# First batch's q and k transposed by half rows, pair 0's masks moved behind its keys, token weights moved ahead of values 3, and mode changes counted when the order is planned

## The chip, the cores and the metric

The kernel runs on one core of a Trainium2 chip. The core has a matmul engine (PE, whose weight loads are listed apart as PEld), a vector engine (DVE), a scalar engine (ACT), a general engine (POOL, which here also issues most loads and makes their descriptors in software) and a queue engine (SP, which issues the first loads and all stores). The metric is the device time of one execution in microseconds (us), as the median of several.

## What is computed

Attention with a sliding window of 128 keys and four "sink" keys that everyone sees, for 4 batches, 8 heads, 768 positions and 64 columns a head; its output, heads side by side as 512 columns, goes into an MLP mixer. Cut to what matters:

```python
scores = (q @ k.T) / sqrt(D)
keep = (pos_k < n_sink) | ((pos_q - pos_k >= 0) & (pos_q - pos_k < window))
x = softmax(where(keep, scores, -1e9)) @ v            # heads become columns: x is 768 x 512
h = relu(x.T @ w_tok1) @ w_tok2                       # token mixing, 768 -> 256 -> 768
u = x + h.T
out = u + relu(u @ w_ch1) @ w_ch2                     # channel mixing, 512 -> 1536 -> 512
```

## The kernel before, in words

**Tiling.** Two heads make a pair; 4 batches of 4 pairs give pairs 0 to 15. For a pair, q and k (128 rows by 6 blocks by 2 heads by 64 columns) are cast to bfloat16, transposed by PE into PSUM, and evicted to qT and kT by ACT or DVE. The two heads lie on the two halves of the 128 rows, so a score matmul contracts 64 rows and the two heads' matmuls use different halves of the array. Scores are made transposed, in three groups g of two key tiles each, so that exp(scores) is at once the stationary operand pT of the values matmul. Here "64-row" or "half-row" work is a matmul or transpose that uses half of the array's rows, and "128-row" work one that uses all.

**Masks.** For batch 0, `masked` (line 469) first writes large negative numbers into the score bank by a 128-row matmul of `mask_add` with the identity, two matmuls a group, and the scores accumulate on top. For later batches DVE multiplies pT by a 0/1 mask after the exponential (line 510).

**Sinks.** `score_sinks` (line 527) scores the sink keys of two pairs at once; their exponentials are pT_sink. `pv` (line 548) makes the values of half a pair with its sums, and DVE divides (recip, line 567, and norm, line 571).

**PSUM.** Two double banks called "sc" hold scores; four banks called "mx" hold everything else: transposes, sink scores, values, token mixing and channel mixing.

**Token and channel mixing.** `mix_h` and `mix_u` (lines 668 and 696) do token mixing for column groups g = 0 (pairs 0 and 1 of a batch) and g = 1 (pairs 2 and 3); u comes either by a DVE add of x or, with `by_pe`, by one more matmul of x with the identity, after which ACT or DVE only copies. u is transposed (`transpose_u`, line 757), and `mix_channels` (line 849) multiplies by w_ch1 and w_ch2.

**Transposes.** For batch 0 and for pair 4, `transpose_whole` (line 430) turns q or k by six 128-row transposes into one "mx" bank. For pair 0 it also issues 3 (q) and 4 (k) matmuls of a tile of ones, whose result nobody reads (`keep_warm`, line 138); seven more such matmuls open the kernel. From pair 5 on, `transposed` (line 448) turns q and k by 12 half-row transposes each, in one "sc" bank, in the same burst as the pair's first scores.

**What sets the order.** The instructions' order on every engine is worked out while the kernel is built. `Plan` (line 236) holds when each engine is free by a table of costs; units of PE work have dependencies and PSUM banks (`unit`, line 352; `burst`, line 361, puts pieces together and adds 190 ns). `Plan.run` (line 306) takes, among the lists of batch 0 (scores, masks, transposes, values, token mixing of g = 1, of g = 0), the first that can start within 40 ns of the soonest; after that the channel units ("main") and the later batches' attention and token units ("side") alternate, so that the side keeps to `target` (line 1022), a share of its total size. Evictions and other work go to the engine that ends first, and `urgent` settles ties. POOL's queue of loads follows the order of the `queue` calls (lines 961 to 1000): values 1, 2, 3, then w_tok1, w_tok2, then pair 4, two pieces of w_ch1, pair 5, and so on; at most 8 loads are under way. The plan's landing time of a weight load counts 2000 ns for it in the queue (`load_weights`, line 953).

Of the kernel before, what the change touches and what calls it, by code (L numbers as in the profile page):

```python
# [16 lines left out]
def kernel(  # L17
# [13 lines left out]
    nc = tc.nc  # L31
# [14 lines left out]
    NQ = 6  # L46
    MASKED_BY_PE = 4

# [163 lines left out]
    SEM = 90.0  # L212
    PE_OUT = 190.0
    FIRST = 1800.0
    LANES = 8
# [5 lines left out]
    class Op:  # L221
        def __init__(self, cost, fn, deps=(), then=(), size=0.0, lag=None, loads=0):
            self.cost, self.fn, self.deps, self.then = cost, fn, list(deps), list(then)
            self.done = None
            self.lag = SEM if lag is None else lag
            self.size = size
            self.urgent = 0
            self.loads = loads
            self.need = {}

    def landed(at):
# [4 lines left out]
    class Plan:  # L236
        def __init__(self):
            self.free = {"PE": 0.0, "ACT": 0.0, "DVE": 0.0, "SP": 0.0, "POOL": 0.0}
            self.queue, self.landings = 0.0, []
            self.pending = []  # L240
            self.held = {t: [()] * n for t, n in TAGS.items()}
# [54 lines left out]
        def commit_pe(self, op, t):  # L296
            for tag, banks in op.need.items():
                given[tag] = [n for _, n in self.slots(tag)[:len(banks)]]
                for n, readers in zip(given[tag], banks):
                    self.held[tag][n] = readers  # L300
            op.fn()
            self.free["PE"] = t + op.cost["PE"]
            op.done = self.free["PE"] + PE_OUT + SEM
            self.pending.extend(op.then)

        def run(self, first, main, side, target):
# [3 lines left out]
            while any(first) or main or side or self.pending:  # L310
# [40 lines left out]

    def unit(ns, fn, deps=(), need=None, then=()):
# [5 lines left out]
        op.need = need or {}  # L358
        return op

    def burst(*pieces):
# [6 lines left out]
        def run():  # L368
# [19 lines left out]
    def prepare(p):  # L388

        kT, ks = kTb[p % NKB], kTs[p % NHP]  # L390
        parts = 2 if p < NHP else 1

        def evict(e, n, part):
            name = ("q", "k")[n]
            if n:
                t = kT
            elif ("qT", p) in tiles:
                t = tiles["qT", p]
            else:
                t = tiles["qT", p] = att_pool.tile([P, S], BF16, name="qT2")  # L400
            view, ps = tiles["ps_" + name, p]
            to = view(t)
            if parts == 2:
                ps, to = ps[:, ts(part, P // 2)], to[:, ts(part, P // 2)]
            copy(e, to, ps)

        def sink_columns(e):
            c = ODD * (p % 2)
            ps = tiles["ps_k", p][1]
            first = ps[:, 0, 0:n_sink] if len(ps.shape) == 3 else ps[:, 0, 0, 0:n_sink]  # L410
            for i in range(2):
# [7 lines left out]
        for n, name in enumerate(("qT", "kT")):  # L419
# [3 lines left out]
            for part, op in enumerate(done[name, p]):  # L423
                op.urgent = (3 - part if parts == 2 else 0)
        tiles["kT", p] = kT
# [3 lines left out]

    def transpose_whole(p, n):  # L430

        name = ("q", "k")[n]

        def run():
            ps = bank("mx", NT, P, dtype=BF16)
            tiles["ps_" + name, p] = (
                lambda t: t.rearrange("d (p j) -> d p j", j=NT), ps.rearrange("d j p -> d p j"),
            )
# [5 lines left out]
        then = done[name + "T", p] + ([done["kTs", p]] if n else [])  # L444
        done["t" + name, p] = unit(340, run, [done[name + "_bf", p]], {"mx": [then]}, then)
        return done["t" + name, p]

    def transposed(p):

        def run():  # L450
            ps = bank("sc", 2, 8 * P, dtype=BF16)[:, :, 0:2 * NT * D].rearrange("d x (n j p) -> d x n j p", n=2, j=NT)
            for n in range(2):
                for j in range(NT):
                    for x in range(2):
                        rows = ds(D * x, D)
                        in_order(nc.tensor.transpose(ps[:, x, n, j], bfs[p, n][rows, j], ident[rows, rows]))  # L456
                tiles["ps_" + "qk"[n], p] = (
                    lambda t: t.rearrange("d (x p j) -> d x p j", x=2, j=NT), ps[:, :, n].rearrange("d x j p -> d x p j"),
                )
# [9 lines left out]
    def masked(p, g):  # L469
# [78 lines left out]
    def pv(p, half):  # L548
# [230 lines left out]
    def first_attention():  # L779

        for p in range(NHP):
            prepare(p)
        turned = [transpose_whole(p, n) for p in range(NHP) for n in range(2)]
        masks, scored, out = [], [], []
        for p in range(NHP):
            for g in range(NT // 2):
                if p < MASKED_BY_PE:
                    masks.append(masked(p, g))
                if g == 0 or p < MASKED_BY_PE:
                    scored.append(burst(scores(p, g)))  # L790
                elif g == 1:
                    scored.append(burst(scores(p, 1), scores(p, 2)))
                if g == 0 and p == NHP - 1:
# [6 lines left out]
        for g in range(2):  # L800
            tokens.append([mix_h(0, g, t, 1) for t in range(NTOK)] if g else [mix_h(0, g, 0, NTOK)])
            tokens[g] += [mix_u(0, g, st, 2, st == 2) for st in range(0, NT, 2)]
            tokens[g] += [transpose_u(0, g, st, 2) for st in range(0, NT, 2)]
        return scored, masks, turned, out, *tokens[::-1]

    def attention_and_tokens():
# [3 lines left out]
        prepare(first)  # L810
        units += [transpose_whole(first, n) for n in range(2)]
        for p in range(first, last + 1):
# [140 lines left out]
    def load_weights(fn):  # L953
        return Op({"POOL": 760.0}, lambda e: fn(), lag=2000.0, loads=1)

# [114 lines left out]
```

## Time and profile before

| | us |
|---|---|
| median of 3 executions | 211.01 |
| lowest, highest | 210.95, 213.33 |
| profiled execution, device time | 211.41 |
| its span, first to last instruction | 209.6 |

How to read the lines below: a line of the timeline gives the start, the time until the end of the last instruction of the group, engine, source line, operation and "out<-in" by tile names, the shape and the count; in brackets stands how long the engine idled before it and what ended that. Since matmuls are pipelined, the time of one includes its way through the array; the spacing of starts is what one costs. A line of the stretches gives busy time and instruction count by engine. A line of the DMA view gives a load's size and the time from issue to landing. The chain is followed back from the last instruction, at each step to what released it.

### The profile page before, as it was taken

To read this page: it belongs to the slowest core of one execution; us is meant where nothing else is said; L and a number is where in the kernel's file an instruction comes from. 1 tells how busy PE (TensorE), PEld (TensorE's weight loads), DVE (VectorE), ACT (ScalarE), POOL (GpSimd) and SP (SyncE) were. 2 spreads that over 40 slices of the span, in tenths; PEclk is the share of its full clock that TensorE was granted. 3 is DMA by queue.
4 is the path that set the end of the run, shared out by engine and by line. 5 is a ranking of instruction groups with operands and counts; after the bars stand their busy time and mean duration, and the time that the engine had idled before them with its cause. 6 is when DMAs were issued, how large, how long until landed. Compare 5 with 4: busy or idle time off the path is not lost.

```text
span 209.6 us, 4916 instructions
## 1 busy us (share of the span) xinstructions
PE 200.8 (96%) x2071; PEld 122.2 (58%) x2090; DVE 114.7 (55%) x250; ACT 112.6 (54%) x200; POOL 67.4 (32%) x86
## 2 busy tenths in 40 slices
PE   7999999999999998999999999999999999999994
PEld 2555786565656565657656554666766545565443
DVE  4687554657677758876586452776663522000222
ACT  4697667958726435966684340968581102774000
POOL 6199849696599990630000000000000000000000
PEclk9999999999999999999999999999999999999999
DMA  6999999999999999793000212100001122000222
GB/s 193 281 250 177 170 177 189 150 146 195 165 172 194 184 185 199 52 83 27 0 3 2 103 50 100 53 0 5 0 3 50 50 103 100 0 0 3 100 100 100
DMA packets 73221, 21.55 MB, mean 103 GB/s; under 512 B 63216, under 2 KB 70256, under 8 KB 73200
## 3 DMA queue, kind: packets, MB, share of 16 engines
q0 software_dynamic: 67232, 11.80, 71.8%
q1 hardware_dynamic: 5968, 9.45, 12.7%
q8 instruction: 16, 0.26, 0.5%
q14 instruction: 5, 0.04, 0.1%
HBM read 26.75 MB, written 6.29 MB: 158 GB/s over the span
## 4 chain that ended last, share of the span: by engine, by line
PE 90%; ACT 5%; DVE 3%; issue 1%; ACTq 0%
PE ps_mx L109 77%; PE ps_sc L109 8%; PE ps_mx L112 2%; DVE kT L118 2%; PE ps_sc L456 2%; ACT qT L116 2%; ACT v1T L122 1%; ACT pT L506 1%; PE ps_mx L742 1%; ACT kTs L116 1%; DVE u_sb L713 0%; DVE ones L136 0%; PE ps_sc L742 0%; DVE o_sb L920 0%; ACTq L116 0%
## 5 line engine op out<-in xcount | busy, mean ns | idle before, releaser
L109 PE MATMUL ps_mx<-uT,w_ch 128*128 128x384 bf16 x384 | 67.4, 326 | 1.0 <-ACT v1T L122 0.9
L109 PE MATMUL ps_mx<-w_ch,v1T 128*128 128x512 bf16 (+2 forms) x298 | 64.4, 362 | 0.8 <-issue 0.2
L122 ACT ACTIVATE v1T<-ps_mx 128x384 bf16<-128x384 f32 x73 | 35.8, 492 | 30.4 <-PE ps_mx L109 20.1
L109 PEld LDWEIGHTS <-w_ch 128*128 128x128 bf16 x384 | 36.2, 98 | 24.8 <-issue 2.0
L109 PEld LDWEIGHTS <-v1T 128*128 128x128 bf16 x312 | 29.1, 98 | 29.5
L506 ACT ACTIVATE pT<-ps_sc 128x1024 bf16<-128x1024 f32 (+1 forms) x48 | 44.1, 951 | 2.9 <-PE ps_sc L109 2.6
L884 DVE TENSOR_TENSOR o_sb<-ps_mx,u_sb 128x512 f32<-128x512 f32 x23 | 15.9, 690 | 41.4 <-PE ps_mx L109 41.4
L94 POOL DMA_DIRECT2D q_bf<-in_q_dram x24 | 19.7, 823 | 4.4 <-DMA w_ch<-in_moe_w_ch_dram 2.3
L109 PEld LDWEIGHTS <-w_tok 128*128 128x128 bf16 x192 | 18.4, 98 | 4.3 <-issue 0.5
L94 POOL DMA_DIRECT2D k_bf<-in_k_dram x24 | 19.6, 820 | 3.3 <-DMA w_ch<-in_moe_w_ch_dram 1.7
L102 POOL DMA_DIRECT2D v_aug<-in_v_dram x16 | 16.7, 1042 | 9.7 <-PE ps_mx L109 7.0
L713 DVE TENSOR_TENSOR u_sb<-ps_mx,x_sb 128x512 bf16<-128x512 f32 x22 | 14.1, 685 | 8.7 <-PE ps_mx L109 8.7
L118 DVE COPY kT<-ps_sc 128x768 bf16<-128x768 bf16 x11 | 10.5, 958 | 13.1 <-ACT qT L116 13.1
L124 DVE TENSOR_SCALAR v1T<-ps_mx 128x384 bf16<-128x384 f32 x23 | 12.8, 555 | 6.7 <-PE ps_mx L109 6.5
L109 PE MATMUL ps_sc<-qT,kT 64*128 64x256 bf16 x192 | 15.6, 263 | 0.5 <-ACT pT L506 0.2
L513 DVE TENSOR_TENSOR pT<-pT,mask_main 128x1024 bf16<-128x1024 bf16 (+1 forms) x24 | 14.2, 619 | 2.4 <-ACT pT L506 2.4
L109 PE MATMUL ps_mx<-v_aug,pT 128*128 128x65 bf16 x352 | 14.9, 194 | 0.0
L109 PEld LDWEIGHTS <-pT 128*128 128x128 bf16 x352 | 13.3, 97 | 1.7 <-DVE recip L569 0.2
L116 ACT ACTIVATE qT<-ps_sc 128x768 bf16<-128x768 bf16 x11 | 8.9, 810 | 9.8 <-PE ps_sc L456 9.7
L109 PE MATMUL ps_mx<-h1T,w_tok 128*128 128x256 bf16 x96 | 12.4, 273 | 0.0
L109 PE MATMUL ps_mx<-x_sb,w_tok 128*128 128x256 bf16 x96 | 11.8, 273 | 0.0
L612 DVE TENSOR_TENSOR x_sb<-ps_mx,recip 128x384 bf16<-128x384 f32 x22 | 11.5, 552 | 0.1
(71 smaller groups left out, 154.6 us busy)
## 6 DMA issues: line engine op xcount, KB each, us to landing
out_dram<-o_sb SPq DMA_DIRECT2D x23, 256.0 KB, 2.0
v_aug<-in_v_dram POOLq DMA_DIRECT2D x16, 192.0 KB, 6.8
w_ch<-in_moe_w_ch_dram POOLq DMA_DIRECT2D x8, 384.0 KB, 9.1
q_bf<-in_q_dram POOLq DMA_DIRECT2D x24, 96.0 KB, 6.8
k_bf<-in_k_dram POOLq DMA_DIRECT2D x24, 96.0 KB, 5.8
q_f<-in_q_dram SPq DMA_DIRECT2D x4, 384.0 KB, 6.1
k_f<-in_k_dram SPq DMA_DIRECT2D x4, 384.0 KB, 6.4
w_tok<-in_moe_w_tok_dram POOLq DMA_DIRECT2D x2, 384.0 KB, 7.6
```

What stands on the lines that cost most here:

```text
L94: in_order(nc.gpsimd.dma_start(out=out[:, h], in_=rows[:, h]))
L102: in_order(nc.gpsimd.dma_start(out=v_aug.rearrange("p i t d -> p (i t) d")[:, :, 0:D], in_=v[b].rearrange("h s d -> (h s) d")[2 * hp * S:2 ...
L109: in_order(nc.tensor.matmul(*args, skip_group_check=True, **kwargs))
L116: in_order(nc.scalar.activation(out, in_, AF.Copy))
L118: in_order({"DVE": nc.vector, "POOL": nc.gpsimd}[e].tensor_copy(out=out, in_=in_))
L122: in_order(nc.scalar.activation(out, in_, AF.Relu))
L124: in_order(nc.vector.tensor_scalar_max(out=out, in0=in_, scalar1=0.0))
L506: in_order(nc.scalar.activation(part(tiles["pT", p][:, :, ds(2 * g, 2)]), tiles["ps_s", p, g][:, :, 0:width(g)], AF.Exp, scale=scale,))
L513: in_order(nc.vector.tensor_tensor(out=pt, in0=pt, in1=m, op=ALU.mult))
L612: in_order(nc.vector.tensor_tensor(out=x_sb[b][:, :, ds((2 * hp + i) * D, D)], in0=tiles["ps_o", p, i][:, :, 0:D], in1=tiles["recip", p, i ...
L713: in_order(nc.vector.tensor_tensor(out=u_part(b, g, s0, n), in0=tiles["ps_u", b, g, s0], in1=x_sb[b][:, s0:s0 + n, c0:c0 + cn], op=ALU.add,))
L884: in_order(nc.vector.tensor_tensor(out=o_sb.rearrange("p (g c) -> p g c", g=2), in1=u_rows(b, st), in0=tiles["ps_out", b, st].rearrange("p ...
```

## The change

- `turn` takes the place of `transpose_whole`: q or k of a pair of batch 0 and of pair 4 is turned by twelve half-row transposes into two "mx" banks, one for each half of the rows, and each half has its own eviction. Pair 4's evictions come in two parts as well. The 3 and 4 matmuls on ones go.
- The masks of pair 0 depend on its k transposes, so they are placed behind them; group 0 of pair 3 loses its mask matmuls and is masked by DVE.
- The plan adds 95 ns (SWITCH) at each change between half-row and 128-row work, in place of 190 ns a burst, and prefers to stay with half-row work if it can start within 95 ns. `transposed` counts 350 instead of 430, `turn` 180.
- In batch 0, `mix_h` of g = 0 goes in two units, and all three `mix_u` units of g = 0 add x on PE (before: one of the three).
- The recip and norm of pairs 2 and 3 rank higher.
- w_tok1 is loaded before values 3, and weight loads count 1700 ns in the plan.

```diff
-    MASKED_BY_PE = 4
+    MASKED_BY_PE = [(p, g) for p in range(NHP) for g in range(NT // 2) if (p, g) != (NHP - 1, 0)]
...
+    SWITCH = 95.0
...
-            self.free["PE"] = t + op.cost["PE"]
+            self.free["PE"] = t + op.cost["PE"] + SWITCH * (op.half != self.half)
+            self.half = op.half
...
-                    t, u = next(((t, u) for t, u in early if t <= soonest + 40.0), (None, None))
+                    stay = [(t, u) for t, u in early if self.half and u[0].half and t <= soonest + SWITCH]
+                    t, u = next((e for e in stay + early if e[0] <= soonest + (SWITCH if e in stay else 40.0)), (None, None))
...
-            190 + sum(p.size for p in pieces), run, [d for p in pieces for d in p.deps], need,
-            [t for p in pieces for t in p.then],
+            sum(p.size for p in pieces), run, [d for p in pieces for d in p.deps], need,
+            [t for p in pieces for t in p.then], half=True,
...
-        parts = 2 if p < NHP else 1
+        parts = 2 if p <= NHP else 1
...
-    def transpose_whole(p, n):
+    def turn(p, n):
...
-            ps = bank("mx", NT, P, dtype=BF16)
...
+            ps = [bank("mx", NT, D, dtype=BF16) for _ in range(2)]
+            tiles["ps_" + name, p] = [t.rearrange("d j p -> d p j") for t in ps]
             for j in range(NT):
-                transpose(ps[:, j], bfs[p, n][:, j])
-            if p == 0:
-                keep_warm(3 + n, plan.spare())
...
+                for x in range(2):
+                    rows = ds(D * x, D)
+                    in_order(nc.tensor.transpose(ps[x][:, j], bfs[p, n][rows, j], ident[rows, rows]))
+
+        readers = [[op] for op in done[name + "T", p]]
+        if n:
+            readers[0].append(done["kTs", p])
+        done["t" + name, p] = unit(
+            180, run, [done[name + "_bf", p]], {"mx": readers}, [op for r in readers for op in r], half=True,
+        )
...
-            430, run, [done["q_bf", p], done["k_bf", p]], {"sc": [then]}, then, [("tq", p), ("tk", p)],
+            350, run, [done["q_bf", p], done["k_bf", p]], {"sc": [then]}, then, [("tq", p), ("tk", p)],
...
-        done["mask", p, g] = unit(width(g) * 0.84, run, [], {"sc": [[x]]})
+        deps = [done["tk", 0]] if p == 0 else []
+        done["mask", p, g] = unit(width(g) * 0.84, run, deps, {"sc": [[x]]})
...
-        n.urgent = r.urgent = p < NHP
+        n.urgent = r.urgent = (1 + 1.5 * (p >= NHP // 2)) * (p < NHP)
...
-            tokens.append([mix_h(0, g, t, 1) for t in range(NTOK)] if g else [mix_h(0, g, 0, NTOK)])
-            tokens[g] += [mix_u(0, g, st, 2, st == 2) for st in range(0, NT, 2)]
+            tokens.append([mix_h(0, g, t, 1) for t in range(NTOK)])
+            tokens[g] += [mix_u(0, g, st, 2, g == 0 or st == 2) for st in range(0, NT, 2)]
...
-        return Op({"POOL": 760.0}, lambda e: fn(), lag=2000.0, loads=1)
+        return Op({"POOL": 760.0}, lambda e: fn(), lag=1700.0, loads=1)
...
         queue(("v", p), load_values(p))
+        if p == NHP - 2:
+            queue("tok1", load_weights(lambda: load_w(w_tok1, moe_w_tok1.rearrange("(t p) n -> p t n", p=P))))
     done["v", 1].deps.append(v_sink)
-
-    queue("tok1", load_weights(lambda: load_w(w_tok1, moe_w_tok1.rearrange("(t p) n -> p t n", p=P))))
```

More of the change, by code (lines that the diff above doesn't have):

```diff
@@ L229, in __init__ @@
             self.need = {}
+            self.half = False
     def landed(at):
@@ L239, in __init__ @@
             self.queue, self.landings = 0.0, []
+            self.half = False
             self.pending = []
@@ L350, in run, with unit @@
                 self.commit_pe(op, t)
-    def unit(ns, fn, deps=(), need=None, then=()):
+    def unit(ns, fn, deps=(), need=None, then=(), half=False):
         op = Op({"PE": float(ns)}, fn, deps, then, size=float(ns))
@@ L358, in unit @@
         op.need = need or {}
+        op.half = half
         return op
@@ L400, in evict @@
                 t = tiles["qT", p] = att_pool.tile([P, S], BF16, name="qT2")
[L401 to L405, printed above, removed]
+            to = t.rearrange("d (x p j) -> d x p j", x=2, j=NT)
+            copy(e, to if parts == 1 else to[:, part], tiles["ps_" + name, p] if parts == 1 else tiles["ps_" + name, p][part])
         def sink_columns(e):
             c = ODD * (p % 2)
-            ps = tiles["ps_k", p][1]
-            first = ps[:, 0, 0:n_sink] if len(ps.shape) == 3 else ps[:, 0, 0, 0:n_sink]
+            first = (tiles["ps_k", p][:, 0] if parts == 1 else tiles["ps_k", p][0])[:, 0, 0:n_sink]
             for i in range(2):
@@ L423, in prepare @@
             for part, op in enumerate(done[name, p]):
-                op.urgent = (3 - part if parts == 2 else 0)
+                op.urgent = (3 - part) * (p < NHP)
         tiles["kT", p] = kT
@@ L428, in prepare @@
         )
-    def transpose_whole(p, n):
+    def turn(p, n):
         name = ("q", "k")[n]
         def run():
-            ps = bank("mx", NT, P, dtype=BF16)
-            tiles["ps_" + name, p] = (
-                lambda t: t.rearrange("d (p j) -> d p j", j=NT), ps.rearrange("d j p -> d p j"),
-            )
+            ps = [bank("mx", NT, D, dtype=BF16) for _ in range(2)]
+            tiles["ps_" + name, p] = [t.rearrange("d j p -> d p j") for t in ps]
             for j in range(NT):
-                transpose(ps[:, j], bfs[p, n][:, j])
-            if p == 0:
-                keep_warm(3 + n, plan.spare())
-        then = done[name + "T", p] + ([done["kTs", p]] if n else [])
-        done["t" + name, p] = unit(340, run, [done[name + "_bf", p]], {"mx": [then]}, then)
+                for x in range(2):
[7 more added lines that the diff above has]
+        )
         return done["t" + name, p]
@@ L456, in run @@
                         in_order(nc.tensor.transpose(ps[:, x, n, j], bfs[p, n][rows, j], ident[rows, rows]))
-                tiles["ps_" + "qk"[n], p] = (
-                    lambda t: t.rearrange("d (x p j) -> d x p j", x=2, j=NT), ps[:, :, n].rearrange("d x j p -> d x p j"),
-                )
+                tiles["ps_" + "qk"[n], p] = ps[:, :, n].rearrange("d x j p -> d x p j")
         then = [*done["qT", p], *done["kT", p], done["kTs", p]]
         return piece(
-            430, run, [done["q_bf", p], done["k_bf", p]], {"sc": [then]}, then, [("tq", p), ("tk", p)],
+            350, run, [done["q_bf", p], done["k_bf", p]], {"sc": [then]}, then, [("tq", p), ("tk", p)],
         )
@@ L782, in first_attention @@
             prepare(p)
-        turned = [transpose_whole(p, n) for p in range(NHP) for n in range(2)]
+        turned = [turn(p, n) for p in range(NHP) for n in range(2)]
         masks, scored, out = [], [], []
@@ L786, in first_attention @@
             for g in range(NT // 2):
-                if p < MASKED_BY_PE:
+                if (p, g) in MASKED_BY_PE:
                     masks.append(masked(p, g))
[L789 to L792, printed above, removed]
+                scored.append(burst(scores(p, g)))
                 if g == 0 and p == NHP - 1:
@@ L810, in attention_and_tokens @@
         prepare(first)
-        units += [transpose_whole(first, n) for n in range(2)]
+        units += [turn(first, n) for n in range(2)]
         for p in range(first, last + 1):
```

## The prediction

> **What bounds the kernel now.** I read the page first (busy shares, then the chain), then busy time by stretches that I cut where the work changes.
>
> ```profile
> PE 200.8 (96%) x2071; PEld 122.2 (58%) x2090; DVE 114.7 (55%) x250; ACT 112.6 (54%) x200; POOL 67.4 (32%) x86
> PE 90%; ACT 5%; DVE 3%; issue 1%; ACTq 0%
> ```
>
> ```profile
> 0.00:4.63 4.63, 3.17 (x8) 1.20 (x9) 2.28 (x14) 1.97 (x2) 3.26 (x10) 1.00 0.57 184
> 4.63:8.40 3.77, 3.71 (x25) 1.66 (x23) 2.00 (x7) 1.40 (x5) 0.06 (x1) 1.00 1.29 259
> 8.40:23.63 15.23, 14.43 (x196) 8.76 (x199) 10.99 (x29) 13.63 (x21) 13.45 (x16) 1.00 1.77 218
> 23.63:32.20 8.57, 8.45 (x109) 7.62 (x105) 5.46 (x13) 5.08 (x10) 5.25 (x8) 1.00 1.90 178
> 32.20:209.60 177.40, 171.04 (x1747) 102.98 (x1760) 93.98 (x190) 90.53 (x166) 45.36 (x54) 1.00 0.72 84
> ```
>
> Columns of the second fence: stretch, its length, then busy time (and count) of PE, PEld, DVE, ACT, POOL, then clock, DMA share and rate. PE has work 96% of the span and 90% of the chain that ended last. The channel stage with the later batches' side work, 177.40 us, keeps its instructions apart from two transposes of pair 4; only its order can move. What the change rewrites lies before 32.20: the head up to the first scores (8.40), the attention of batch 0 (15.23 us, PE busy 14.43, ACT 13.63), and its token mixing (8.57 us, PE busy 8.45). So the question is by how much the channel stage starts earlier, and whether its 177.40 us stay.
>
> **The head (masks of pair 0 moved, warm-up matmuls removed).**
>
> ```profile
> 1.46 3.17 PE L109 MATMUL ps_mx<-ones 128*128 128x512 bf16 x7 [1.46 <-DVE ones L136]
> 3.94 0.84 ACT L116 ACTIVATE q_bf<-q_f 128x768 bf16<-128x768 f32 x1 [1.92 <-DMA q_f<-in_q_dram]
> 4.43 1.64 PE L109 MATMUL ps_sc<-mask_add,ident 128*128 128x512 bf16 x4
> 4.92 0.56 DVE L118 CAST k_bf<-k_f 128x768 bf16<-128x768 f32 x1 [1.44 <-DMA k_f<-in_k_dram]
> 5.91 0.50 PE L112 MATMUL ps_mx<-ident,q_bf 128*128 128x128 bf16 x6
> 7.11 0.49 PE L112 MATMUL ps_mx<-ident,k_bf 128*128 128x128 bf16 x6
> 7.44 1.03 PE L109 MATMUL ps_mx<-ones 128*128 128x512 bf16 x4
> 7.64 0.87 ACT L116 ACTIVATE kT<-ps_mx 128x384 bf16<-128x384 bf16 x2 [0.71 <-PE ps_mx L112]
> 8.40 0.61 PE L109 MATMUL ps_sc<-qT,kT 64*128 64x256 bf16 x8
> ```
>
> q is cast at 3.94+0.84 = 4.78, but its transposes start at 5.91: PE works in order, and four mask matmuls stand ahead. k is cast at 5.48, but is transposed at 7.11, behind q's transposes and three warm-up matmuls. These are 1.1 and 1.6 us. After the change k's transposes can start at about 5.6. Twelve half-row transposes take 0.18 us at full clock (below), so k is done by 5.8. Then come the four masks of groups (0,0) and (0,1), at 0.21 us each (below) 0.86 us, and a mode change of 0.1 us on either side: 6.9. Beside the masks runs k's eviction: here it begins 0.53 us after its transposes and one half takes 0.49, so it would end near 6.6 and hides under them; without that cover the scores still wait only for 6.7. With 0.1 for a semaphore, first scores at 7.0 against 8.40: 1.4 us gained. The seven warm-up matmuls themselves filled waits, so they add nothing to that.
>
> The other bound is the clock. The column of granted clock says 1.00 throughout, but the seven 512-column matmuls from 1.46 to 4.43 stand 0.42 us apart, and the masks from 4.43 to 5.91 fit three at 0.42 and one at 0.21; so full rate comes at about 5.7, after 4.2 us without a hole. The change opens a hole from 4.43 to 4.87. If the masks still run at 0.42 us, they end 0.84 us later: scores at 7.9, gain 0.5. I take 7.0, because of those 4.2 us about 3 were dense already and the transposes resume 0.4 us later; 0.5 is kept for the range.
>
> [...]
>
> **The attention of batch 0.**
>
> ```profile
> 10.23 0.50 PE L112 MATMUL ps_mx<-ident,k_bf 128*128 128x128 bf16 x6
> 10.66 0.34 PE L109 MATMUL ps_sc<-qT,kT 64*128 64x256 bf16 x4
> 11.47 0.39 PE L109 MATMUL ps_sc<-qT,kT 64*128 64x256 bf16 x4
> 20.80 0.59 PE L109 MATMUL ps_sc<-mask_add,ident 128*128 128x512 bf16 x2
> 21.32 0.39 PE L109 MATMUL ps_sc<-qT,kT 64*128 64x256 bf16 x4
> 34.90 0.35 PE L456 MATMUL ps_sc<-ident,q_bf 64*128 64x64 bf16 x12
> 35.08 0.34 PE L456 MATMUL ps_sc<-ident,k_bf 64*128 64x64 bf16 x12
> 35.26 0.38 PE L109 MATMUL ps_sc<-qT,kT 64*128 64x256 bf16 x4
> 22.55 0.20 DVE L569 RECIPROCAL recip<-ps_mx 128x6 f32<-128x6 f32 x1 [1.94 <-PE ps_mx L109]
> ```
>
> A busy time includes the pipeline's tail, so I price PE from start to start. Six whole transposes then scores: 10.23 to 10.66, 0.43 us, of which 0.10 is the change into half rows; so 0.33. Twelve half-row ones: 34.90 to 35.08, 0.18. Two masks and a mode change: 20.80 to 21.32, 0.52, so 0.21 a mask. A half-row turn beside scores saves 0.15; one standing alone pays two mode changes, 0.20, and loses 0.05. For q and k of pairs 1 to 3 and of pair 4 that is eight turns: between +0.4 (none adjacent) and -1.2 us (all). I take half adjacent, -0.4.
>
> Mask group (3,0) leaves PE: two matmuls, -0.43. It becomes a DVE multiply of about 0.7 us after its exponential; DVE idles 1.94 us before the reciprocal at 22.55 and is busy 10.99 of 15.23, so I price it at nothing; uncovered it costs those 0.7.
>
> Each turn now takes two of the four "mx" banks, one per half, freed by its own eviction. q and k of one pair fill all four, and values, sink scores and token mixing wait for one. An eviction is 0.49 us in the row of kT: 0 to 1.0 us over three pairs; I take 0.2.
>
> The head's 1.4 us must survive the arrivals of later pairs.
>
> ```profile
> 2.25 0.47 SPq L81 DMA_DIRECT2D k_f<-in_k_dram  x1
> 4.92 0.48 SPq L81 DMA_DIRECT2D k_f<-in_k_dram  x1
> 12.03 1.27 POOL L102 DMA_DIRECT2D v_aug<-in_v_dram  x1
> 13.29 0.83 POOL L127 DMA_DIRECT2D w_tok<-in_moe_w_tok_dram  x1
> ```
>
> ```profile
> k_f<-in_k_dram SPq DMA_DIRECT2D x1, 384.0 KB, 6.3
> ```
>
> ```profile
> k_f<-in_k_dram SPq DMA_DIRECT2D x1, 384.0 KB, 7.6
> ```
>
> ```profile
> v_aug<-in_v_dram POOLq DMA_DIRECT2D x1, 192.0 KB, 7.5
> ```
>
> k of pair 1 is issued at 2.25 and lands at 8.55; cast 0.56, turn with its latency 0.4, eviction 0.49: scores (1,0) at 10.0 at the earliest, against 11.47, which keeps 1.4. k of pair 2 lands at 4.92+7.6 = 12.5, so its scores can't come before 14.0; PE has scores and masks of pair 1 to do until about 13.2, and values need the sink exponential. I take 0.3 us lost, between 0 and 1.0. Values 3 and the first token weights swap on POOL's queue: values 3 go out 0.83 us later and land at 12.03+0.83+7.5 = 20.4, before pair 3's values at some 21.5, so nothing; were they due before, up to 0.8. SP's queue is untouched, and what follows on POOL keeps its time.
>
> **Token mixing.**
>
> ```profile
> 26.24 0.27 PE L109 MATMUL ps_mx<-x_sb,ident 128*128 128x256 bf16 x1
> 26.35 0.38 PE L109 MATMUL ps_mx<-h1T,w_tok 128*128 128x256 bf16 x2
> 32.20 2.76 PE L109 MATMUL ps_mx<-uT,w_ch 128*128 128x384 bf16 x16
> ```
>
> The first group's residual moves to PE for four more blocks, 26.24 to 26.35 each: +0.44. In return ACT or DVE may empty them. Splitting h by halves and the higher rank of pairs 2 and 3's norms shorten waits in a stretch where PE idles 0.12 us by its row: 0 to -0.3, I take -0.1.
>
> **The later order.** A burst's 190 becomes two changes of 95, so its price in the plan stays, but target() now sees smaller side units, and the plan believes weights land 0.3 us earlier each, 1.2 us by pair 5's keys. PE idles 177.40-171.04 = 6.4 us there; a changed order can move a tenth of that either way: 0, within 0.6.
>
> **Sum.** -1.4 head, -0.4 turns, -0.43 mask, +0.2 banks, +0.3 arrivals, +0.44 residual, -0.1 waits: -1.4 us. The profiled execution took 211.41 us, 1.8 around its span of 209.6, so 210.0; it stands 0.4 above the median 211.01, so the median would be 209.6. The gain has a ceiling.
>
> ```profile
> 20.62 1.53 POOL L127 DMA_DIRECT2D w_ch<-in_moe_w_ch_dram  x2
> ```
>
> ```profile
> w_ch<-in_moe_w_ch_dram POOLq DMA_DIRECT2D x1, 384.0 KB, 8.9
> ```
>
> The first channel weights land at 20.62+8.9 = 29.5, so 32.20 can't move by more than 2.7 us.
>
> **The rivals.** *Late clock:* the count of 4.2 us begins again at 5.6, so full rate comes at 9.8. Speaking for it: nothing here shows that a hole is forgiven; against: 3 dense us stand before it. Some 2.4 us of matmuls would double there (six masks 1.2, pair 0's scores 0.7, turns 0.5); from 5.6 to the earliest scores (1,0) at 10.0 PE has 4.4 us for these 2.4 and for 0.8 of mode changes, so 1.2 are hidden and 1.2 are not: 210.8. [...] *Clock that stays low:* the holes between pair 0's scores and pair 1's keys break the second count too, and half rate lasts to about 14. PE has 14.43 of 15.23 us busy there, so the 4.2 us more cost 2.1, and 212.9 results, slower than before; it decides from a full rate after about 10.2, where the 1.4 are used up. *The change moves nothing:* turns stand alone (+0.8 against my sum), and the banks (+0.8 at their bound) hold up values: 211.2; for it speaks that ACT is busy 13.63 of 15.23 and evicts too. *More:* all turns adjacent (-0.8), no arrival lost (-0.3), a better later order (-0.6): 207.9, near the ceiling.
>
> **How the numbers follow.** Forecast 0.50 (its own range 208.9 to 210.3), late clock 0.16, clock that stays low 0.13, nothing moved 0.13, more 0.08. The predicted time is the forecast's. The range 208.2 to 212.5 leaves out most of "more" and the worse half of the low clock with a later order gone wrong, together under 0.2. Two per cent, 4.2 us, is about what a measurement of this kernel can tell from no change: faster would need more than the ceiling, 0.03; slower needs the low clock to last beyond 18 us, 0.06; within, 0.91.
>
> **What would show it.** Head: scores of pair 0 at 7.0 (right), 7.9 or later (clock), and the masks after the keys 0.21 or 0.42 us apart. Turns: half-row transposes next to 64-row scores, or with 128-row work on both sides. Banks and arrivals: scores (1,0) near 10.0, scores (2,0) near 14.5 against 16.4. Tokens: the first channel matmul near 30.8. Later order: the stretch after it 177.4 us long, within 0.6; if it grows by 1.4 the prediction is wrong though every early step is right.

## The result, and the profile after

The changed kernel takes 209.94 us (median of 14 executions, 209.46 to 210.52) against 211.77 before (14 executions, 210.95 to 213.56): a ratio of 0.991, 95% interval 0.9886 to 0.9934. In us that is 1.4 to 2.4 less. The forecast was 1.4 less, all of it ahead of the channel stage. Of the kernels below, `no_stay` was profiled in an execution of 517.42 us, where its other five took 209.25 to 209.88; that profile isn't used.

The page after, the lines that answer to the two shown of before:

```profile
PE 198.0 (95%) x2126; PEld 119.3 (57%) x2145; DVE 114.3 (55%) x252; ACT 114.4 (55%) x202; POOL 67.5 (32%) x86
PE 83%; DMA 6%; DVE 4%; ACT 2%; issue 2%; POOL 1%; SPq 0%; POOLq 0%; DVEq 0%
```

PE is still the bound, but in this execution the chain runs through DMA for 6% of the span: it no longer goes back to the first matmuls, but over the sink values and the first token weights to the first token matmul, which waits for them until 19.27. Busy time by stretches, cut at the first scores, the first token matmul, and the first channel matmul:

```profile
0.00:4.63 4.63, 3.17 (x7) 0.89 (x7) 2.28 (x14) 2.08 (x2) 3.26 (x10) 1.00 0.59 183
4.63:7.65 3.02, 1.76 (x29) 0.92 (x30) 1.69 (x7) 1.79 (x5) 0.06 (x1) 1.00 1.25 273
7.65:19.27 11.62, 10.29 (x181) 5.61 (x183) 9.50 (x24) 10.94 (x18) 10.81 (x13) 1.00 1.66 244
19.27:30.78 11.51, 11.34 (x157) 9.47 (x157) 6.65 (x16) 7.74 (x13) 7.91 (x11) 1.00 1.92 175
30.78:207.70 176.92, 171.41 (x1762) 102.43 (x1772) 94.20 (x192) 91.83 (x167) 45.41 (x54) 1.00 0.73 85
```

The first channel matmul moves from 32.20 to 30.78, the 1.4 us of the forecast, and the stretch behind it from 177.40 to 176.92. That stretch also took over the turn of pair 4's k, as the PE timeline shows:

```profile
30.50 0.35 PE L442 MATMUL ps_mx<-ident,q_bf 64*128 64x64 bf16 x12
30.78 1.47 PE L109 MATMUL ps_mx<-uT,w_ch 128*128 128x384 bf16 x8
32.18 0.35 PE L442 MATMUL ps_mx<-ident,k_bf 64*128 64x64 bf16 x12
32.47 1.47 PE L109 MATMUL ps_mx<-uT,w_ch 128*128 128x384 bf16 x8
```

The turn and its two mode changes take 32.47-32.18 = 0.29 us. Before, the same turn stood ahead of the channel stage, at 31.86, for 0.34 us. So counted alike (pair 4's k behind), the first batch ends at 30.78 against 31.86, 1.1 us sooner. For the later stage I measure from the first channel matmul of the first batch to that of the fourth, first before, then after:

```profile
32.20:175.32 143.12, 139.78 (x1557) 85.20 (x1569) 88.82 (x181) 78.76 (x142) 45.36 (x54) 1.00 0.86 91
```

```profile
30.78:173.36 142.58, 140.15 (x1572) 84.67 (x1581) 89.04 (x183) 80.06 (x143) 45.41 (x54) 1.00 0.87 92
```

With 0.29 taken off for the turn this is 142.29, 0.8 us less. So the gain has two parts: 1.1 us in the first batch and 0.8 us in a stage in which the change touches little but the order. Both come from one profile of each kernel; that of the kernel before wasn't taken again.

### The profile page after: what moved, and what is told of

It reads as the page before. It is cut to its first block, busy times and chain, and to the rows that moved or that the text cites. A ratio compares the mean times of both kernels' runs of the same rounds, so it can differ in the third digit from the quotient of the medians.

```text
span 207.7 us, 5034 instructions
## 1 busy us (share of the span) xinstructions
PE 198.0 (95%) x2126; PEld 119.3 (57%) x2145; DVE 114.3 (55%) x252; ACT 114.4 (55%) x202; POOL 67.5 (32%) x86
## 4 chain that ended last, share of the span: by engine, by line
PE 83%; DMA 6%; DVE 4%; ACT 2%; issue 2%; POOL 1%; SPq 0%; POOLq 0%; DVEq 0%
PE ps_mx L109 75%; PE ps_sc L109 5%; DMA w_tok<-in_moe_w_tok_dram 4%; DMA v_sink_f<-in_v_dram 2%; PE ps_sc L460 2%; DVE x_sb L615 1%; ACT qT L116 1%; DVE kT L118 1%; POOL v_aug L102 1%; PE ps_mx L745 1%; ACT v1T L122 1%; DVE recip L612 1%; PE ps_mx L112 1%; POOL v_sink L118 0%; SPq L188 0%
## 5 line engine op out<-in xcount | busy, mean ns | idle before, releaser
L109 PE MATMUL ps_mx<-uT,w_ch 128*128 128x384 bf16 x384 | 68.3, 326 | 0.9 <-DVE x_sb L615 0.9
L122 ACT ACTIVATE v1T<-ps_mx 128x384 bf16<-128x384 f32 x74 | 36.3, 493 | 33.7 <-PE ps_mx L109 22.9
L109 PEld LDWEIGHTS <-w_ch 128*128 128x128 bf16 x384 | 35.5, 98 | 25.0 <-DVE x_sb L615 2.5
L94 POOL DMA_DIRECT2D k_bf<-in_k_dram x24 | 19.6, 820 | 3.1 <-DMA w_ch<-in_moe_w_ch_dram 1.7
L716 DVE TENSOR_TENSOR u_sb<-ps_mx,x_sb 128x512 bf16<-128x512 f32 x20 | 12.7, 685 | 4.2 <-PE ps_mx L109 4.2
L124 DVE TENSOR_SCALAR v1T<-ps_mx 128x384 bf16<-128x384 f32 x22 | 12.1, 554 | 2.7 <-PE ps_mx L109 2.0
```

The costliest lines, as they stand in the source:

```text
L94: in_order(nc.gpsimd.dma_start(out=out[:, h], in_=rows[:, h]))
L109: in_order(nc.tensor.matmul(*args, skip_group_check=True, **kwargs))
L122: in_order(nc.scalar.activation(out, in_, AF.Relu))
L124: in_order(nc.vector.tensor_scalar_max(out=out, in0=in_, scalar1=0.0))
L716: in_order(nc.vector.tensor_tensor(out=u_part(b, g, s0, n), in0=tiles["ps_u", b, g, s0], in1=x_sb[b][:, s0:s0 + n, c0:c0 + cn], op=ALU.add,))
```

## The experiments

All are timed against the kernel before on the same chip; the ratio's 95% interval stands in brackets. The profiles of kernels with the changed kernel's first batch have the first channel matmul between 30.53 and 31.18, which is the spread from one execution to the next. "Counted alike" means with pair 4's q turned ahead of that matmul and its k behind it.

### The yardstick

The changed kernel again, unedited.

> The changed kernel once more, as the yardstick for the kernels run with it. Both theories: 209.9 us, first channel matmul near 30.8 us; what differs from the first profile (first scores at 7.65, stretch after the first channel matmul 176.92 us long) is the spread of one execution to the next.

209.81 us, ratio 0.9886 (0.9841 to 0.9931). First channel matmul 31.06; first to fourth batch 142.60. The later stage repeats to 0.02 us, the first batch to 0.3. What varies most is the head. PE in the first profile, then in this one:

```profile
4.78 0.50 PE L442 MATMUL ps_mx<-ident,q_bf 64*128 64x64 bf16 x12
6.40 0.35 PE L442 MATMUL ps_mx<-ident,k_bf 64*128 64x64 bf16 x12 [1.11 <-DVE k_bf L118]
6.68 1.04 PE L109 MATMUL ps_sc<-mask_add,ident 128*128 128x512 bf16 x4
7.65 0.61 PE L109 MATMUL ps_sc<-qT,kT 64*128 64x256 bf16 x8
```

```profile
4.92 0.50 PE L442 MATMUL ps_mx<-ident,q_bf 64*128 64x64 bf16 x12 [0.29 <-ACT q_bf L116]
5.70 0.50 PE L442 MATMUL ps_mx<-ident,k_bf 64*128 64x64 bf16 x12 [0.28 <-DVE k_bf L118]
6.13 1.89 PE L109 MATMUL ps_sc<-mask_add,ident 128*128 128x512 bf16 x4
7.95 1.03 PE L109 MATMUL ps_sc<-qT,kT 64*128 64x256 bf16 x8
```

In the first, k is late (its cast ends at 6.34, 0.9 us after the forecast's 5.48), and four masks fit 6.68 to 7.65, full rate. In the second, k is nearly on time, but the masks need 6.13 to 7.95, some 0.43 us each: half rate. So k's data came late in the one and the clock in the other, and the first scores lie 0.3 us apart. In the first profile the token weights then hold PE up as well: they were issued at 11.33 and took 7.9 us, to 19.2, while in the yardstick they land at 11.59+7.1 = 18.7 and PE comes to them at 19.57. Its chain goes through the head, with 2% of DMA.

### Does the head carry?

```diff
-        deps = [done["tk", 0]] if p == 0 else []
-        done["mask", p, g] = unit(width(g) * 0.84, run, deps, {"sc": [[x]]})
+        done["mask", p, g] = unit(width(g) * 0.84, run, [], {"sc": [[x]]})
...
+            if p == 0:
+                keep_warm(3 + n, plan.spare())
```

> Undoes the head alone: masks of pair 0 free to go first again, and 3 and 4 warm-up matmuls behind q and k of pair 0. Theory 'less work' (the gain came from work that left PE between pair 1's first scores, at 11.41 against 11.47 before, and the channel stage): first scores move back by 0.7 to 1.4 us, but what counts is what PE has done when pair 1's keys arrive, so the first channel matmul moves from 30.8 to at most 31.2, and the time to 209.9 to 210.4. Rival 'head carries' (the forecast's 1.4 us of the head reach the end): first channel matmul at 31.8 to 32.2, time 211.0 to 211.3.

210.2 us, 0.9896 (0.9855 to 0.9936). First scores at 8.48, but the first channel matmul at 30.90, with both of pair 4's turns behind it, which makes it 31.2 counted like the others. The scores come 0.5 us after the yardstick's and 0.8 after the first profile's, the channel stage 0.1 and 0.4 after theirs. So "head carries" falls, as far as it lets the whole 1.4 us through, and the numbers of "less work" hold; but a part of the head arrives, and the yardstick hides some of it, since its own masks ran at half rate.

```diff
-    keep_warm(7, 0)
```

> As changed, without the seven warm-up matmuls that open the kernel. Tells what the clock needs. [...]

210.33 us, 0.9924 (0.9893 to 0.9955). PE of this kernel:

```profile
6.04 1.89 PE L109 MATMUL ps_sc<-mask_add,ident 128*128 128x512 bf16 x4
7.86 1.03 PE L109 MATMUL ps_sc<-qT,kT 64*128 64x256 bf16 x8
9.58 0.80 PE L109 MATMUL ps_sc<-mask_add,ident 128*128 128x384 bf16 x2 [0.37 <-ACT pT L508]
```

The masks run at half rate, and so do the two at 9.58 (0.80 us where the yardstick's two at 9.68 take 0.48). The first channel matmul is at 31.01 beside the yardstick's 31.06, and the fourth batch starts at 173.60 beside 173.66. That doesn't make the clock free, for the yardstick's masks ran at half rate too. Six profiles have this order of the first batch; from their PE timelines:

| profile | first scores | first token matmul | first channel matmul |
|---|---|---|---|
| `size_back` (below) | 7.40 | 19.03 | 30.53 |
| the first of the changed kernel | 7.65 | 19.27 | 30.78 |
| `price_430` (below) | 7.78 | 19.40 | 30.90 |
| `results_later` (below) | 7.79 | 19.69 | 31.18 |
| `warm0` | 7.86 | 19.51 | 31.01 |
| yardstick | 7.95 | 19.57 | 31.06 |

From the first token matmul on, all six take 11.5 us, so the end of the first batch is set by when that matmul starts. In the last four the masks stay at half rate (1.82 us from the first of the four to the scores). Three of these, whose chains go back through PE's head, end 0.4 to 0.5 us after `size_back`, whose masks got faster on the way (1.50 us). The chains of `size_back` and `results_later` go through the load of pair 2's k (its cast ends at 12.92 and 13.59), that of the first profile through the token weights. So the first batch ends by the latest of three paths, PE's head, pair 2's k and the token weights, that lie close together: a late head is passed on, an early one only until a load takes over. The times agree: the seven executions without the warm-up (209.99 to 210.69) all lie above the six of `size_back` (208.85 to 209.84) and the five of `no_stay` (209.25 to 209.88), which were timed beside them on the same chip.

### What do the half-row turns give?

```diff
-            ps = [bank("mx", NT, D, dtype=BF16) for _ in range(2)]
+            ps = bank("mx", NT, P, dtype=BF16)
...
-                for x in range(2):
-                    rows = ds(D * x, D)
-                    in_order(nc.tensor.transpose(ps[x][:, j], bfs[p, n][rows, j], ident[rows, rows]))
+                transpose(ps[:, j], bfs[p, n][:, j])
...
-        done["t" + name, p] = unit(
-            180, run, [done[name + "_bf", p]], {"mx": readers}, [op for r in readers for op in r], half=True,
-        )
+        done["t" + name, p] = unit(340, run, [done[name + "_bf", p]], {"mx": [then]}, then)
```

> Turns q and k of pairs 0 to 4 by six 128-row transposes again, everything else as changed. Theory 'less work': six turns of pairs 1 to 3, all next to scores in the changed kernel, cost 0.15 us more each, so the first channel matmul comes 0.6 to 1.2 us later, 31.4 to 32.0, and the time is 210.5 to 211.1. Rival 'head carries' with waits for arrivals and banks as the bound: two banks less per pair in use, no change or 0.3 us faster, 209.6 to 209.9.

209.96 us, 0.9886 (0.9846 to 0.9927): no difference in time. The first channel matmul comes at 31.80 with pair 4's k ahead of it at 30.84, so 31.46 counted alike: 0.4 us after the yardstick, 0.3 beyond the spread. Since its masks ran at nearly full rate (6.08 to 7.15), the profiles with a faster head are the fairer measure, and after those, 30.78 and 30.53, it is 0.7 and 0.9. Its later stage takes 142.07, 0.2 less than the yardstick's without pair 4's k. So whole turns cost the first batch 0.4 to 0.9 us, and the time doesn't show it; neither theory gave both.

### What does the counting of mode changes give?

```diff
-    SWITCH = 95.0
+    SWITCH = 0.0
...
-                    stay = [(t, u) for t, u in early if self.half and u[0].half and t <= soonest + SWITCH]
-                    t, u = next((e for e in stay + early if e[0] <= soonest + (SWITCH if e in stay else 40.0)), (None, None))
+                    t, u = next(((t, u) for t, u in early if t <= soonest + 40.0), (None, None))
...
-            sum(p.size for p in pieces), run, [d for p in pieces for d in p.deps], need,
+            190 + sum(p.size for p in pieces), run, [d for p in pieces for d in p.deps], need,
...
-            350, run, [done["q_bf", p], done["k_bf", p]], {"sc": [then]}, then, [("tq", p), ("tk", p)],
+            430, run, [done["q_bf", p], done["k_bf", p]], {"sc": [then]}, then, [("tq", p), ("tk", p)],
```

> Takes the counting of mode changes out of the order: SWITCH 0, 190 ns a burst, no preference for staying with half-row work, 430 for a later pair's transposes; weight loads keep 1700. Theory 'less work': turns no longer stand next to scores, each pays two mode changes, 0.2 us, so the first channel matmul comes 0.6 to 1.2 us later; the stretch behind it goes from 176.9 back to about 177.4 if its shortening came from the order. Rival: turns and scores meet without it, and the later stretch shortened by chance: 209.9 within 0.3.

212.06 us, 0.9995 (0.9968 to 1.0022): the whole gain is gone, though all the other edits stand. First scores come at 7.07, the earliest of all, but the first channel matmul at 31.89, and

```profile
31.89:175.34 143.45, 140.20 (x1571) 85.31 (x1581) 88.76 (x177) 80.10 (x149) 44.43 (x53) 1.00 0.85 91
```

is 0.85 us longer than the yardstick's 142.60. The expected reason fails for the first batch: three of the four turns of pairs 2 and 3 still stand directly ahead of scores (k of pair 2 at 13.20 and scores at 13.38, and so on). What it lost lies later: its last two score groups start at 22.02 and 23.14, the yardstick's together at 21.07.

The counting alone, on the kernel before (the edit is the reverse of the last one, with burst marked as half-row and without `turn`):

> The kernel before with the counting of mode changes alone: 95 ns at each change between half-row and 128-row bursts in place of 190 a burst, the preference to stay, 350 for a later pair's transposes. Whole transposes, masks, loads and token mixing as before. Theory 'order' (the counting gives the later stage its shorter waits, and the first batch gains by its other parts only together with it): from first to fourth batch's first channel matmul about 142.3 in place of 143.1 us, first channel matmul near 32, time 0.8 to 1.2 us under before. Rival 'parts' (the counting does nothing without half-row turns): as before within 0.3.

211.28 us, 0.9975 (0.9948 to 1.0002). First to fourth batch takes 142.17 in place of 143.12, but the first channel matmul comes at 32.80 in place of 32.20: 0.95 gained behind, 0.6 lost ahead. So the later part of the gain is the counting's alone; the first needs it together with the other edits.

The preference to stay, taken out alone:

```diff
-                    stay = [(t, u) for t, u in early if self.half and u[0].half and t <= soonest + SWITCH]
-                    t, u = next((e for e in stay + early if e[0] <= soonest + (SWITCH if e in stay else 40.0)), (None, None))
+                    t, u = next(((t, u) for t, u in early if t <= soonest + 40.0), (None, None))
```

> As changed, but without the preference to stay with half-row work in the first batch; mode changes are still priced. Theory 'order': turns of pairs 1 to 3 drift away from the scores, each costs 0.2 us more of mode changes, so the end of the first batch comes 0.5 to 1.0 us later and the time is 210.3 to 210.9. Rival: the price of 95 alone keeps them together, 209.8 to 210.0.

209.6 us, 0.9895 (0.9864 to 0.9925): it does nothing that the time shows; the price of 95 is enough.

### Through what does the counting shorten the later stage?

Three ways were open: the side units' sizes, the 80 ns less for a later pair's transposes, and the 95 ns that moved from ahead of a burst to behind it.

```diff
+        op.size += 190.0 + 80.0 * any(p.keys and p.keys[0][0] == "tq" for p in pieces)
```

> As changed, but a burst's size, by which the side units keep to their share of the channel work, is again 190 larger and 80 more with a later pair's transposes; its price on PE stays as changed. Theory 'pace' (the later stage is shorter because the smaller sizes move the side units against the channel units): the later waits return, first to fourth batch 143.1 us, time 0.8 us up, 210.6 to 210.9. Rival 'price' (the counted mode changes themselves do it): 142.3 and 209.8 to 210.0 as changed.

209.15 us, 0.9882 (0.9849 to 0.9914). First to fourth batch 172.99-30.53 = 142.46, as with the small sizes: "pace" falls. It is the lowest median here, but its interval covers the yardstick's ratio, so it isn't shown to be a better version.

```diff
-            350, run, [done["q_bf", p], done["k_bf", p]], {"sc": [then]}, then, [("tq", p), ("tk", p)],
+            430, run, [done["q_bf", p], done["k_bf", p]], {"sc": [then]}, then, [("tq", p), ("tk", p)],
```

> As changed, but a later pair's two transposes count 430 again in the plan, not 350; a burst is still two mode changes of 95. Only the later stage's order can differ. Theory 'price' in its narrow form (what shortened the later waits is that a burst's results are expected earlier, by 95 ns from the mode change behind it and by 80 from this number): taking the 80 back brings back part of the waits for v1's evictions on ACT, 0.2 to 0.6 us, so first to fourth batch is 142.8 to 143.2 in place of 142.6. Rival: the 95 alone do it, 142.6 and the same time, 209.8.

209.68 us, 0.9912 (0.9881 to 0.9942). 173.38-30.90 = 142.48: the 80 ns do nothing, the rival is right.

```diff
-            op.done = self.free["PE"] + PE_OUT + SEM
+            op.done = self.free["PE"] + PE_OUT + SEM + 95.0 * (op.half and self.later)
...
+                self.later = not any(first)
```

> As changed, but once the first batch's units are all placed, the plan expects the results of half-row bursts 95 ns later, as it did when a burst's 190 stood ahead of them; PE's own times in the plan stay. The first batch's order is the same as in the changed kernel. Theory 'expected results' (the later stage is shorter because exponentials and evictions are expected 95 ns earlier and so are placed ahead of v1's evictions, or these go to DVE): first to fourth batch's first channel matmul 143.0 to 143.5 in place of 142.5, the waits for ACT's v1 evictions return, time 210.4 to 210.8. Rival 'mode change behind' (the 95 charged to the unit after the burst do it): 142.5 and 209.8 as changed.

210.55 us, 0.9933 (0.9899 to 0.9966), with the first channel matmul at 31.18 and

```profile
31.18:174.55 143.37, 141.38 (x1586) 85.22 (x1581) 88.32 (x179) 80.34 (x147) 45.24 (x54) 1.00 0.86 92
```

The 0.8 us are back in this profile, from one number that only says when a burst's results may be expected; the time is higher too, but its interval overlaps the yardstick's. Beside it `price_430`, the other one whose trace has all matmuls, or nearly:

```profile
30.90:173.38 142.48, 141.30 (x1587) 84.65 (x1582) 89.02 (x181) 79.86 (x145) 45.63 (x54) 1.00 0.88 93
```

PE idles 1.18 us in the latter and 1.99 in the former: 0.81 of the 0.89 us by which the stages differ. It isn't the chance of one order either. Counted alike, the ten profiles of kernels that count mode changes and expect a burst's results early take 142.3 to 142.8 us for the stage; the kernel before, `plan_back` and `results_later` take 143.4 to 143.5.

The waits of PE in the later stage, in us with their count and the longest: the kernel before, the changed kernel, the one with late results. (The first two traces lack some matmuls, 1557 and 1572 where 1586 are recorded in the third; a gap so left can show as "issue".)

```profile
PE ps_mx L109 <- ACT v1T L122: 1.7, 4, 0.4
PE ps_sc L456 <- ACT pT L506: 0.6, 1, 0.6
PE ps_sc L109 <- ACT pT L506: 0.2, 1, 0.2
PE ps_mx L109 <- issue: 0.2, 1, 0.2
```

```profile
PE ps_mx L109 <- DVE x_sb L615: 1.3, 5, 0.4
PE ps_mx L109 <- issue: 0.3, 2, 0.2
```

```profile
PE ps_mx L109 <- ACT v1T L122: 1.7, 4, 0.4
PE ps_mx L109 <- DVE x_sb L616: 0.2, 1, 0.2
```

How this comes about can be seen behind a burst of a side pair. The timeline of one such place, first before, then after (only ACT's and PE's lines):

```profile
46.69 0.49 ACT L122 ACTIVATE v1T<-ps_mx 128x384 bf16<-128x384 f32 x1
...
47.07 1.02 ACT L506 ACTIVATE pT<-ps_sc 128x1024 bf16<-128x1024 f32 x1
47.23 1.46 PE L109 MATMUL ps_mx<-uT,w_ch 128*128 128x384 bf16 x8 [0.43 <-ACT v1T L122]
...
48.62 0.56 PE L109 MATMUL ps_sc<-qT,kT 64*128 64x256 bf16 x8
```

```profile
44.36 1.02 ACT L509 ACTIVATE pT<-ps_sc 128x1024 bf16<-128x1024 f32 x1
...
44.71 0.82 PE L109 MATMUL ps_mx<-uT,w_ch 128*128 128x384 bf16 x4 [0.24 <-DVE x_sb L615]
...
45.28 0.48 ACT L122 ACTIVATE v1T<-ps_mx 128x384 bf16<-128x384 f32 x1
...
45.46 0.56 PE L109 MATMUL ps_sc<-qT,kT 64*128 64x256 bf16 x8
```

Before, ACT empties a bank of v1 first and does the exponential after it; PE waits 0.43 us for that bank and does eight channel matmuls until the next scores. After, the exponential is first, the v1 eviction goes behind it, PE waits 0.24 us for another bank, and the next scores come four matmuls sooner. The kernel with late results has the old rows again: eviction, then exponential, and a wait of 0.43 on ACT.

### The loads and the residual

```diff
+    queue("tok1", load_weights(lambda: load_w(w_tok1, moe_w_tok1.rearrange("(t p) n -> p t n", p=P))))
...
-        if p == NHP - 2:
-            queue("tok1", load_weights(lambda: load_w(w_tok1, moe_w_tok1.rearrange("(t p) n -> p t n", p=P))))
```

> As changed, but the first token weights are loaded behind values 3 again. The forecast's term: nothing, since both are landed when they are used. In the changed kernel the token weights land at 18.7 to 19.2 and the first token matmul starts at 19.3 to 19.6, so a load issued 1.0 us later lands at about 20.1 and the first unit of h must wait or be placed later. Theory 'covered': PE has other work then, first channel matmul within 0.2 us of 31.06, time 209.8. Rival 'the load is the bound': first channel matmul 0.5 to 0.9 us later, time 210.4 to 210.7.

210.36 us, 0.9936 (0.9915 to 0.9958). PE's first token matmuls, after, then here, with the first channel matmul of the latter:

```profile
19.27 0.83 PE L109 MATMUL ps_mx<-x_sb,w_tok 128*128 128x256 bf16 x6
```

```profile
21.41 0.82 PE L109 MATMUL ps_mx<-x_sb,w_tok 128*128 128x256 bf16 x6
...
32.06 0.47 PE L442 MATMUL ps_mx<-ident,k_bf 64*128 64x64 bf16 x12
32.59 0.65 PE L109 MATMUL ps_mx<-uT,w_ch 128*128 128x384 bf16 x3
```

The weights land at 12.44+8.6 = 21.0 in place of 18.7 in the yardstick, the first token matmul starts 2.1 us after the changed kernel's, and the first batch ends at 32.59 with pair 4's k ahead: 32.06 counted alike, 1.0 us after the yardstick's 31.06. 0.45 of it arises before the orders part, at the scores of 18.93 (the yardstick's are at 18.48), where pair 2's k is late again; the other 0.55 is the swap's. "The load is the bound" has the right numbers, though PE doesn't wait for the weights here: the plan expects them later and places scores and masks first. The later stage hid none of it (174.60 against 173.66).

```diff
-            tokens[g] += [mix_u(0, g, st, 2, g == 0 or st == 2) for st in range(0, NT, 2)]
+            tokens[g] += [mix_u(0, g, st, 2, st == 2) for st in range(0, NT, 2)]
```

> As changed, but the first group's u adds x by PE in one of three units again, by DVE in two. The forecast's term: four identity matmuls less, 0.44 us of PE. Theory 'PE-bound tokens': first channel matmul 0.3 to 0.45 us earlier, 30.6 beside 31.06 in the yardstick, time 209.4. Rival 'DVE in the way' (the two adds stand behind the norms of pairs 2 and 3 on DVE and hold u up): no change or 0.3 us later.

209.98 us, 0.9929 (0.9901 to 0.9957). The first channel matmul is at 31.30 with pair 4's k ahead of it at 31.02, so 31.02 counted alike, as the yardstick. But here the token weights land at 11.56+8.0 = 19.6 and PE waits for them. From the first token matmul at 19.61 it is 11.41 us, against 11.50 in the six profiles above: four matmuls less gain 0.1.

## Why the prediction was right, and where it was right by accident

The direction, the size and the range were right: 209.6 was forecast, 209.94 measured, 1.4 us less forecast, 1.4 to 2.4 measured. But the sum is a sum of misses that cancel, and the closeness of 209.6 to 209.94 is luck in part: the forecast counted from 211.01, the median of three executions, where fourteen give 211.77. It put all of the gain ahead of the channel stage, and 0.8 us of it lie behind.

**The head, -1.4.** This step failed. First scores came at 7.40 to 7.95 in six profiles, not 7.0. The late clock stood in the text as a bound; that k's own landing varies did not. And of what the head gains only a part arrives: with the old head the first batch ends 0.1 us after the yardstick, 0.4 after the first profile and 0.7 after `size_back`. The forecast let pair 1's scores follow its keys, at 10.0. They start at 11.41, against 11.47 before, by PE's timeline:

```profile
9.76 0.33 PE L109 MATMUL ps_sc<-qT,kT 64*128 64x256 bf16 x4
10.46 0.38 PE L109 MATMUL ps_sc<-mask_add,ident 128*128 128x512 bf16 x1 [0.36 <-ACT pT L509]
10.88 0.59 PE L109 MATMUL ps_mx<-qT,kTs 128*128 128x512 bf16 x2
11.41 0.39 PE L109 MATMUL ps_sc<-qT,kT 64*128 64x256 bf16 x4
```

The mask of group (1,0), at 10.46, needs a score bank, which comes free with the second exponential, and ACT evicts pair 1's q between the first and the second:

```profile
9.00 0.49 ACT L116 ACTIVATE qT<-ps_mx 128x384 bf16<-128x384 bf16 x1
9.37 1.03 ACT L509 ACTIVATE pT<-ps_sc 128x1024 bf16<-128x1024 f32 x1
```

The forecast counted PE, the loads and the keys' eviction here, not the order on ACT and the two score banks. What is left of the head at this point of the first profile is that the sink scores, 0.43 us, now stand ahead of pair 1's scores.

**The clock.** It was right to keep it as a bound and wrong in its price. Half rate until after 7.7 (the four masks in 1.82 us) happened in three of the five profiles of this order that have the warm-up. Where nothing else was late it costs 0.4 to 0.5 us of the first batch against `size_back`, not the 1.2 of the rival.

**Turns, -0.4.** About right or too small in the first batch (whole turns: 0.4 to 0.9 us later). Not half, but all six of pairs 1 to 3 stand next to scores; in the time the term doesn't show.

**Token weights before values 3, 0.** This step failed. The text asked only whether values 3 come too late. With all edits the first token matmuls run at 19.27, among pair 3's attention, where before they stood behind it, at 23.63. The swap undone alone puts them at 21.41 and costs 0.55 us of the first batch behind the scores where the orders part.

**Residual, +0.44.** Failed: 0.1 measured. PE does 0.44 us more, and the other way loses most of that elsewhere; where stays open.

**Later order, 0 within 0.6.** Failed: -0.8, outside its bounds. The text looked at the plan's price of PE, which stays the same, and at the sizes, which do nothing; it overlooked that a burst's results are expected when its own price ends, so that 95 ns moved behind it change what ACT does first.

The terms for the mask of pair 3, for the banks and for the shorter waits were not tried alone, and that for the arrivals only as far as the loads above show it. Nor do the parts add up: each was undone alone, in an order worked out anew.

## What to carry to other kernels

A gain ahead of a stage counts only as far as what that stage waits for next moves too: ask for pair 1 which bank, which eviction and which load come last, not only which data. And know the state of the execution that you compare with: a kernel without the warm-up looked as fast as a yardstick whose masks happened to run at half rate (first channel matmul at 31.01 and 31.06). In an order that is planned, a price does two things, it fills an engine and it dates the results; moving 95 ns from ahead of a unit to behind it leaves the first as it was, yet was worth 0.8 us through the order on another engine. And when a load is moved, look at what it sets free as well as at what it delays.

## What the runs showed of the hardware

The matmul rate after a start with a hole isn't the same from one execution to the next: with the same seven warm-up matmuls the four masks took 0.97 us from start to scores in the first profile of the changed kernel and 1.82 in the second; in `price_430` and `results_later` they took 1.82 too, in `size_back` 1.50. The column of granted clock doesn't show such differences: after, it says 1.00 for 0.00 to 4.63, where the warm-up matmuls start 0.43 us apart, and for 4.63 to 7.65, where the masks start 0.22 us apart. Without any warm-up, full rate was reached between the masks at 9.58 and the transposes at 10.31, about 5 us after the first transpose at 4.86. The length of the hole alone doesn't decide between these two profiles: the first has the longer one (1.11 us before k's turn, where the second has 0.28) and reached full rate sooner. The landing of the first k also varies: issued at 1.24 in both, it took 3.7 us before, to 4.9, and 4.5 us in the first profile after, to 5.7.
